# Attention units alternated on VectorE with buffers of their own, mixer tiles re-ordered, and the reciprocal root moved to ScalarE, in a fused attention and gated-MLP block

## The chip, the cores and the metric

The kernel runs on one core of a Trainium2 chip. The metric is the device time of one execution, in microseconds (us). Every comparison below uses executions of both kernels on the same chip in the same rounds. The runs of one kernel lie within 0.7% of each other.

The engines are TensorE (PE in the profile; its weight loads are PEld), VectorE (DVE), ScalarE (ACT), GpSimd (POOL) and SyncE (SP, which issues all DMA transfers of the kernel before, and all but the 16 `o` stores of the kernel after).

## The reference

The input x is 2048 rows by 1024 columns, in bfloat16. The reference, cut to what matters:

```python
def _A_ref(x, wqkv, wo):                 # local dilated attention: 32 heads of 32, window 8, dilation 2
    qkv = (x @ wqkv) ...                 # 1024 -> 3072
    idx = pos[:, None] - off[None, :]    # each row sees itself and 7 earlier rows, two apart
    logits = einsum('bhsd,bhswd->bhsw', q, kg) * scale
    attn = softmax(where(mask, logits, -1e9))
    o = einsum('bhsw,bhswd->bhsd', attn, vg)
    return o @ wo

def _B_ref(x, w_in, w_sp, b_sp, w_out):  # gated MLP with a mix over rows
    z = gelu(x @ w_in)                   # 1024 -> 3584
    z1, z2 = z[..., :1792], layernorm(z[..., 1792:])
    g = einsum('ts,bsf->btf', w_sp, z2) + b_sp[None, :, None]   # 2048 x 2048
    return (z1 * g) @ w_out

h = x + _A_ref(layernorm(x))
out = h + _B_ref(layernorm(h))
```

## The kernel before

There are three stages.

- **Stage A** normalises x, does the QKV matmul for 16 tiles of 128 rows and stores the result to DRAM. VectorE does the attention from there, in 8 "pairs". For each pair it does four QK units (a product and a tree of adds), a softmax with its Exp on ScalarE, and four AV units. The result `o` goes to DRAM.
- **Stage B** works in four blocks of four tiles. Block c needs the attention of pairs 2c and 2c+1. For each tile, S1 transposes the attention result, S2 multiplies by wo and collects statistics, S3 normalises, S4 transposes, S5 computes z2 with gelu, and Z1 computes z1 with gelu.
- **Stage C** mixes over all rows and multiplies by w_out. The change doesn't touch it.

Stages A and B on one side and the attention on the other are two Python generators, "main" and "att". Each `yield t` advances its virtual clock by t, and the generator with the lower clock emits next. That, and then the framework's own scheduler, sets the order in which instructions stand on each engine. The parts that the change touches, cut:

```python
# attention on VectorE
def D1(i):                                     # QK
    for hh in range(2):
        for r in range(2):
            prod = att1.tile([P, W, 512], BF16, name="prod", tag="prod")      # att1: one buffer per tag
            tmp  = att1.tile([P, W, 256], BF16, name="tmp", tag="tmp")
            nc.vector.tensor_tensor(prod[:], qh..., ek[:, r:r + W, :], ALU.mult)              # L482
            nc.vector.tensor_tensor(tmp[:], prod[:, :, 0:256], prod[:, :, 256:512], ALU.add)  # L484
            ...                                # four more halving adds, the last one writes lg
            yield 5.4
def D2(i):                                     # softmax, first half
    nc.vector.tensor_reduce(mx[:], ..., AX.X, ALU.max)
    nc.vector.tensor_tensor(lg[:], lg[:], mx..., ALU.subtract)
    nc.scalar.activation(lg[:], lg[:], AF.Exp)                                # L498
def D3(i):                                     # AV
    pr2 = att1.tile([P, W, 512], BF16, name="pr2", tag="prod")                # the same buffer as prod
    nc.vector.tensor_tensor(pr2..., at..., ev..., ALU.mult)                   # L519
    ...                                        # three halving adds, the last one writes o
    nc.sync.dma_start(dap(o_d[c], ...), os_[r][:])
# order: D1(i), D2(i), D3(i-1), D4(i) (second half of the softmax), D1(i+1), ...

# stage B, in each S2(m), after the matmuls of its tile
nc.scalar.activation(hn[:], h_t[:], AF.Square, bias=nm[:], accum_out=ssq[:])
nc.scalar.activation(ssq[:], ssq[:], AF.Identity, bias=eps_t[:], scale=1.0 / D)
nc.gpsimd.tensor_tensor(rs[:], ssq[:], neghalf[:, 0:1], ALU.pow)              # L365, root on GpSimd
# order in a block: S1 S2 (tile 0), S1 S2 (tile 1), Z1 of two tiles left from the block before,
# S3(0) S4(0) S3(1); then for each tile m: S5(m), S1(m+2), S2(m+2), Z1(m), S4(m+1), S3(m+2)
```

Of the kernel before, what the change touches and what calls it, by code (L numbers as in the profile page):

```python
# [48 lines left out]
def kernel(  # L49
# [12 lines left out]
    nc = tc.nc  # L62
# [26 lines left out]
    mask0 = const.tile([P, 2, W, H], F32, name="mask0")  # L89
# [68 lines left out]
    def gen_main():  # L158
        order = [(c, jj) for c in range(NC) for jj in (0, 2, 1, 3)]
        pbl = abctx.enter_context(tc.tile_pool(name="pbl", bufs=2))  # L160
        with ExitStack() as actx:
# [7 lines left out]
            def Lload(a):  # L169
                if a >= NT:  # L170
                    return
                c, jj = order[a]
                x_t = pa.tile([P, D], BF16, name="x_t", tag="x_t", bufs=6)
                nc.sync.dma_start(x_t[:], dap(x2d, 512 * c + jj, 0, [[4, P], [1, D]]))  # L174
                xts[a] = x_t

            def Lstats(a):
                if a >= NT:
                    return
                xn = pa.tile([P, D], BF16, name="xn", bufs=3)  # L180
# [25 lines left out]
            def Ldve(a):  # L206
# [9 lines left out]
                xn = pa.tile([P, D], BF16, name="xn", bufs=3)  # L216
# [9 lines left out]
            for n in range(1, 6):  # L226
                nc.sync.dma_start(wqkv_sb[:, :, n * 512:(n + 1) * 512], wq_v[:, :, n * 512:(n + 1) * 512])
                if n <= 3:
                    Lload(n + 1)
# [4 lines left out]
            yield 8.0  # L234
# [26 lines left out]
            for a in range(NT):  # L261
                for n in range(6):
                    if n == 0:
                        Lload(a + 5)
                        if a + 2 >= NDVE:
                            Lstats(a + 2)
# [7 lines left out]
                    yield 1.85  # L274
# [15 lines left out]
        with ExitStack() as bctx:  # L290
            wI = bctx.enter_context(tc.tile_pool(name="wI", bufs=1))
            pb = bctx.enter_context(tc.tile_pool(name="pb", bufs=2))
            win1_sb = wI.tile([P, KD, Fh], BF16, name="win1_sb")
            pend_z1 = []

# [11 lines left out]
            for c in range(NC):  # L307
# [8 lines left out]
                ons, xrs, oTs, hts, hns, hTs, ln2, z2s = {}, {}, {}, {}, {}, {}, {}, {}  # L316
                sz = small.tile([P, 4, NFC], F32, name="sz")
                v3 = small.tile([P, 4], F32, name="v3")

                def Bload(m):  # L320
# [3 lines left out]
                    o_n = pbl.tile([P, D], BF16, name="o_n")  # L324
                    nc.sync.dma_start(o_n[:], o_d[c][m * P:(m + 1) * P, :])
                    x_r = pbl.tile([P, D], BF16, name="x_r")
# [9 lines left out]
                def S1(m):  # L336
                    pt = pe_transposes(ons.pop(m))
                    oT = pb.tile([P, KD, P], BF16, name="oT")
                    evac(oT, pt)
                    oTs[m] = oT  # L340

                def S2(m):
                    t = 4 * c + m
                    oT, x_r = oTs.pop(m), xrs.pop(m)
                    h_t = pb.tile([P, D], BF16, name="h_t", bufs=3)
                    hts[m] = h_t
                    s1p = small.tile([P, 2], F32, name="s1p")
                    for n in range(2):
# [4 lines left out]
                        nc.tensor.matmul(ps[:], lhsT=ident[:], rhs=x_r[:, n * 512:(n + 1) * 512], start=False, stop=True)  # L353
                        nc.scalar.activation(h_t[:, n * 512:(n + 1) * 512], ps[:], AF.Identity, accum_out=s1p[:, n:n + 1])
                    nc.sync.dma_start(h_d[t][:, :], h_t[:])
                    Bload(m + 2)
                    nm = small.tile([P, 1], F32, name="nm2")
                    j2 = small.tile([P, 2], F32, name="j2")
                    nc.scalar.activation(j2[:], s1p[:], AF.Identity, scale=-1.0 / D, accum_out=nm[:])
                    hn = pb.tile([P, D], BF16, name="hn")  # L360
                    ssq = small.tile([P, 1], F32, name="ssq2")
                    nc.scalar.activation(hn[:], h_t[:], AF.Square, bias=nm[:], accum_out=ssq[:])
                    nc.scalar.activation(ssq[:], ssq[:], AF.Identity, bias=eps_t[:], scale=1.0 / D)
                    rs = small.tile([P, 1], F32, name="rs2")
                    nc.gpsimd.tensor_tensor(rs[:], ssq[:], neghalf[:, 0:1], ALU.pow)  # L365
                    ln2[m] = (nm, rs, hn)

                def S3(m):
                    nm, rs, hn = ln2.pop(m)
                    nb = small.tile([P, 1], F32, name="nb2")  # L370
                    if last:
                        nc.vector.tensor_tensor(nb[:], nm[:], rs[:], ALU.mult)
                        nc.vector.tensor_scalar(hn[:], hts.pop(m)[:], rs[:], nb[:], ALU.mult, ALU.add)
                    else:
                        nc.scalar.mul(nb[:], nm[:], rs[:])
                        nc.scalar.activation(hn[:], hts.pop(m)[:], AF.Identity, bias=nb[:], scale=rs[:])
                    hns[m] = hn

                def S4(m):
                    pt = pe_transposes(hns.pop(m))  # L380
# [4 lines left out]
                def S5(m):  # L385
                    t = 4 * c + m
                    hT = hTs[m]
                    z2t = z2n[:, t, :] if last else pb.tile([P, ZP], BF16, name="z2s", bufs=4)
                    z2s[m] = z2t
                    for n2 in range(NFC):  # L390
                        ps = ps_mm.tile([P, 512], F32, name="ps", tag="ps")
                        for k in range(KD):
                            nc.tensor.matmul(ps[:, 0:FC], lhsT=hT[:, k, :], rhs=win2_sb[:, k, n2 * FC:(n2 + 1) * FC],  # L393
                                             start=(k == 0), stop=(k == KD - 1))
                        zc = z2t[:, n2 * FC:(n2 + 1) * FC]
# [11 lines left out]
                Bload(0)  # L407
                Bload(1)
# [8 lines left out]
                S2(0)  # L417
                yield 4.5
                S1(1)
                S2(1)  # L420
                yield 4.5
                while pend_z1:
                    yield from Z1(*pend_z1.pop(0))
                S3(0)
                S4(0)
                S3(1)
                yield 1.0
                for m in range(4):
                    yield from S5(m)
                    if m + 2 < 4:  # L430
                        S1(m + 2)
                        S2(m + 2)
                        yield 4.5
# [4 lines left out]
                    if m + 1 < 4:  # L438
                        S4(m + 1)
                        yield 0.6  # L440
                    if m + 2 < 4:
                        S3(m + 2)
                nc.scalar.activation(v3[:], v3[:], AF.Identity, bias=eps_t[:], scale=1.0 / Fh)
                nc.gpsimd.tensor_tensor(rstd3[:, 4 * c:4 * c + 4], v3[:], neghalf[:, 0:4], ALU.pow)  # L444
                yield 1.0
                if last:
                    load_wT(0)
# [4 lines left out]
    def gen_att():  # L452
        NPAIR = 2 * NC
        eks, qhs, evs, lgs, ats = {}, {}, {}, {}, {}

        def loadK(i):
            c, pi = i // 2, i % 2
            base = cls_d[c][pi]
            for hh in range(2):
                qh = att.tile([P, 2, 512], BF16, name="qh")  # L460
                nc.sync.dma_start(qh[:], dap(base, HALO, hh * 512, [[2, P], [1, 2], [1, 512]]))
                ek = att.tile([P, W + 1, 512], BF16, name="ek")
                nc.sync.dma_start(ek[:], dap(base, 0, D + hh * 512, [[2, P], [1, W + 1], [1, 512]]))
                qhs[i, hh], eks[i, hh] = qh, ek

        def loadV(i):
            c, pi = i // 2, i % 2
            base = cls_d[c][pi]
            for hh in range(2):
                ev = att.tile([P, W + 1, 512], BF16, name="ev")  # L470
                nc.sync.dma_start(ev[:], dap(base, 0, 2 * D + hh * 512, [[2, P], [1, W + 1], [1, 512]]))
                evs[i, hh] = ev

        def D1(i):
            lg = att.tile([P, 2, W, H], F32, name="lg")
            lgs[i] = lg
            for hh in range(2):
                qh, ek = qhs.pop((i, hh)), eks.pop((i, hh))
                for r in range(2):
                    prod = att1.tile([P, W, 512], BF16, name="prod", tag="prod")  # L480
                    tmp = att1.tile([P, W, 256], BF16, name="tmp", tag="tmp")
                    nc.vector.tensor_tensor(prod[:], qh[:, r, :].unsqueeze(1).to_broadcast([P, W, 512]),  # L482
                                            ek[:, r:r + W, :], ALU.mult)
                    nc.vector.tensor_tensor(tmp[:], prod[:, :, 0:256], prod[:, :, 256:512], ALU.add)  # L484
                    nc.vector.tensor_tensor(prod[:, :, 0:128], tmp[:, :, 0:128], tmp[:, :, 128:256], ALU.add)  # L485
                    nc.vector.tensor_tensor(tmp[:, :, 0:64], prod[:, :, 0:64], prod[:, :, 64:128], ALU.add)
                    nc.vector.tensor_tensor(prod[:, :, 0:32], tmp[:, :, 0:32], tmp[:, :, 32:64], ALU.add)
                    nc.vector.tensor_tensor(lg[:, r, :, hh * 16:(hh + 1) * 16], prod[:, :, 0:16], prod[:, :, 16:32], ALU.add)
                    yield 5.4

        def D2(i):
# [4 lines left out]
            nc.vector.tensor_reduce(mx[:], lg[:].rearrange("p r j h -> p r h j"), AX.X, ALU.max)  # L496
            nc.vector.tensor_tensor(lg[:], lg[:], mx[:].unsqueeze(2).to_broadcast([P, 2, W, H]), ALU.subtract)
            nc.scalar.activation(lg[:], lg[:], AF.Exp)  # L498
            yield 2.1

        def D4(i):
            lg = lgs.pop(i)
            sm = small.tile([P, 2, H], F32, name="sm")
            nc.vector.tensor_reduce(sm[:], lg[:].rearrange("p r j h -> p r h j"), AX.X, ALU.add)
# [4 lines left out]
            yield 2.4  # L509

        def D3(i):
            c, pi = i // 2, i % 2
            at = ats.pop(i)
            os_ = [att.tile([P, D], BF16, name="o", tag="o", bufs=3) for _ in range(2)]
            for hh in range(2):
                ev = evs.pop((i, hh))
                for r in range(2):
                    pr2 = att1.tile([P, W, 512], BF16, name="pr2", tag="prod")
                    nc.vector.tensor_tensor(pr2[:].rearrange("p j (d hl) -> p j d hl", hl=16),  # L519
# [125 lines left out]
```

## Time and profile before

| what | before | where it is read |
|---|---|---|
| time | 811.31 us, median of 6 (809.84 to 812.87) | runs |
| TensorE busy | 748.7 of 808.0 us | engine table of the page |
| TensorE reaches the last block of stage B | 430.95 us | timeline of TensorE |
| TensorE starts stage C | 513.51 us | timeline of TensorE |
| last attention operation on VectorE | ends at 413.8 us | timeline of VectorE |

The engine table of the page of the kernel before gives busy time, share of the span and number of instructions:

```profile
PE 748.7 (93%) x3936; PEld 372.4 (46%) x3936; DVE 465.8 (58%) x535; ACT 324.6 (40%) x702; POOL 26.8 (3%) x32
```

TensorE is busy nearly all the time, so a gain must come from its gaps and from matmuls that run slowly. The windows view of the same kernel splits the span into the time before the last block of stage B, that block, and stage C. The columns are the window, its length, busy time and instructions of TensorE, its weight loads, VectorE, ScalarE and GpSimd, then the clock that TensorE was granted (1.00 is full speed), the DMA share and GB/s:

```profile
20.00:430.95 410.95, 369.00 (x1960) 181.87 (x1959) 344.15 (x365) 274.75 (x578) 18.32 (x14) 0.96 0.73 235
430.95:513.50 82.55, 80.50 (x457) 41.93 (x456) 14.66 (x19) 46.89 (x121) 4.23 (x6) 1.00 0.38 109
513.50:808.00 294.50, 290.77 (x1472) 143.93 (x1471) 96.67 (x125) 0.00 (x0) 0.00 (x0) 1.00 0.46 116
```

The last two windows have no idle TensorE worth speaking of (2.1 of 82.6 us and 3.7 of 294.5 us). The first has 42 us of it. Its gaps of 2 us and more are in the timeline of TensorE. Columns here and in every timeline are start, duration, engine, line, operation, output and inputs, sizes, count; the bracket has the idle time before it and what ended it:

```profile
98.57 1.03 PE L144 MATMUL pt<-ident,xn 128*128 128x128 bf16 x8 [5.88 <-ACT xn L195]
...
215.25 3.60 PE L351 MATMUL ps<-wo_sb,oT 128*128 128x512 bf16 x8 [13.92 <-DMA win_sb<-in_B_w_in_dram]
...
248.79 6.23 PE L393 MATMUL ps<-win_sb,hT 128*128 128x448 bf16 x32 [3.07 <-ACT hT L148]
...
322.18 7.85 PE L393 MATMUL ps<-win_sb,hT 128*128 128x448 bf16 x32 [2.07 <-ACT hT L148]
...
343.52 1.03 PE L144 MATMUL pt<-ident,hn 128*128 128x128 bf16 x8 [3.10 <-ACT hn L376]
```

For the longest the profile names a DMA of weights that this matmul doesn't read. The timeline of ScalarE shows what held it: the copy that makes `oT`, which the matmul does read, waited 13.1 us for a store of QKV results.

```profile
214.19 1.93 ACT L148 COPY oT<-pt 128x1024 bf16<-128x1024 bf16 x2 [13.09 <-DMA cls_d<-qkv_sb]
```

The timeline of VectorE shows how one QK unit runs. Each operation reads what the one before it wrote:

```profile
128.18 2.29 DVE L482 TENSOR_TENSOR prod<-qh,ek 128x4096 bf16<-128x4096 bf16 x1
130.50 1.23 DVE L484 TENSOR_TENSOR tmp<-prod 128x2048 bf16<-128x2048 bf16 x1
131.76 0.69 DVE L485 TENSOR_TENSOR prod<-tmp 128x1024 bf16<-128x1024 bf16 x1
```

From one start to the next it is 2.32 us for an operation of 2.29 us, and 1.26 us for one of 1.23 us. There is a pause of about 0.03 us after each.

The waits view lists, for an engine's instruction at a line, what it waited for, the total, the number of waits and the longest. Three of its lines for the kernel before:

```profile
PE ps L393 <- ACT hT L148: 11.0, 9, 3.1
ACT lg L498 <- DVE lg L497: 12.2, 5, 7.5
SPq L527 <- DVE o L524: 55.7, 13, 8.4
```

The second is the Exp, waiting for VectorE. The third is the DMA queue holding an `o` store that waits for VectorE.

Last, the groups of instructions by line, for GpSimd: the root in stage B, and the same operation early on, before VectorE is busy.

```profile
L365 POOL TENSOR_TENSOR rs<-ssq,neghalf 128x1 f32<-128x1 f32 x16 | 17.8, 1109 | 380.1 <-ACT ssq L363 363.2 <-issue 16.9
L215 POOL TENSOR_TENSOR brs<-brs,neghalf 128x1 f32<-128x1 f32 x4 | 2.4, 607 | 14.3 <-DVE brs L214 14.3
```

### The profile page before, as it was taken

What the parts mean: (1) busy time and instruction counts of PE and PEld (TensorE: products, weight loads), DVE (VectorE), ACT (ScalarE), POOL (GpSimd) and SP (SyncE); (2) the same over time, 40 slices, a digit from 0 to 9 for tenths busy, and PEclk for the clock granted to TensorE, in tenths of its full rate; (3) what the DMA queues carried; (4) which work ended last, traced back from release to release, by engine and by line L of the source; (5) the groups of instructions that cost most, each with busy time, mean ns of one, the idle gap of its engine ahead of it and who ended that gap; (6) DMA issues with size and microseconds to landing.
All of it is one profiled execution on the core that took longest, in us unless ns stands there. A gap on an engine that the chain in (4) does not pass through costs nothing.

```text
span 808.0 us, 9851 instructions
## 1 busy us (share of the span) xinstructions
PE 748.7 (93%) x3936; PEld 372.4 (46%) x3936; DVE 465.8 (58%) x535; ACT 324.6 (40%) x702; POOL 26.8 (3%) x32
## 2 busy tenths in 40 slices
PE   4899799999388898899999999999999999999998
PEld 2444344444144444444554555444444444444443
DVE  5048899999999999998941000443333333334222
ACT  1857495843197686668677465100000000000000
POOL 2000000000000021101001000000000000000000
PEclk9999899999699999989999999999999999999999
DMA  9669996958796776563649510594443335554111
GB/s 298 187 236 171 368 286 228 316 178 306 280 288 206 235 251 216 184 201 104 231 159 333 153 50 24 200 280 125 108 98 98 97 100 124 119 109 132 42 37 49
DMA packets 144721, 145.58 MB, mean 180 GB/s; under 512 B 69058, under 2 KB 116218, under 8 KB 144676
## 3 DMA queue, kind: packets, MB, share of 16 engines
q1 hardware_dynamic: 144676, 144.97, 59.7%
q8 instruction: 30, 0.49, 0.3%
q14 instruction: 15, 0.12, 0.0%
HBM read 90.97 MB, written 38.24 MB: 160 GB/s over the span
## 4 chain that ended last, share of the span: by engine, by line
PE 59%; DVE 25%; ACT 6%; DMA 5%; SPq 2%; issue 2%; POOL 1%; POOLq 0%; DVEq 0%
PE psg L579 24%; PE pso L598 12%; PE ps L393 9%; DVE prod L482 6%; PE ps L301 5%; DVE pr L519 5%; PE ps L351 4%; PE ps L245 4%; DVE tmp L484 3%; DVE pr L522 2%; DVE prod L485 2%; DMA wqkv_sb<-in_A_wqkv_dram 2%; DVE pr L523 1%; SPq L174 1%; DMA ek<-cls_d 1%
## 5 line engine op out<-in xcount | busy, mean ns | idle before, releaser
L579 PE MATMUL psg<-z2n,wT 128*128 128x448 bf16 (+1 forms) x1024 | 196.4, 353 | 0.6 <-ACT z1s L303 0.6
L245 PE MATMUL ps<-wqkv_sb,xT 128*128 128x512 bf16 x768 | 171.4, 383 | 4.2 <-DMA wqkv_sb<-in_A_wqkv_dram 2.4
L579 PEld LDWEIGHTS <-wT 128*128 128x128 bf16 x1024 | 100.2, 98 | 95.3 <-issue 0.9
L245 PEld LDWEIGHTS <-xT 128*128 128x128 bf16 x768 | 75.2, 99 | 94.5 <-issue 6.5
L393 PE MATMUL ps<-win_sb,hT 128*128 128x448 bf16 x512 | 102.6, 361 | 12.0 <-ACT hT L148 11.0
L583 DVE SCALAR_TENSOR_TENSOR u<-psg,bc,z_c 128x448 bf16<-128x448 f32 x64 | 43.6, 683 | 107.6 <-PE psg L579 101.1
L598 PE MATMUL pso<-wout_sb,uT 128*128 128x512 bf16 x448 | 99.1, 379 | 0.0
L301 PE MATMUL ps<-win_sb,hT 128*128 128x448 bf16 x512 | 98.8, 352 | 0.0
L482 DVE TENSOR_TENSOR prod<-qh,ek 128x4096 bf16<-128x4096 bf16 x32 | 73.4, 2293 | 17.3 <-DMA ek<-cls_d 16.3
L247 ACT ACTIVATE qkv_sb<-ps 128x512 bf16<-128x512 f32 x96 | 54.4, 595 | 60.0 <-PE ps L245 49.8
L393 PEld LDWEIGHTS <-hT 128*128 128x128 bf16 x512 | 50.1, 100 | 61.3 <-ACT hT L148 12.6
L351 PE MATMUL ps<-wo_sb,oT 128*128 128x512 bf16 x256 | 62.5, 388 | 15.8 <-DMA win_sb<-in_B_w_in_dram 13.9
L519 DVE TENSOR_TENSOR pr<-at,ev 128x4096 bf16<-128x4096 bf16 x32 | 73.3, 2289 | 0.7
L301 PEld LDWEIGHTS <-hT 128*128 128x128 bf16 x512 | 50.1, 98 | 47.3
L598 PEld LDWEIGHTS <-uT 128*128 128x128 bf16 x448 | 43.8, 98 | 52.1
L568 DVE TENSOR_TENSOR wT<-wT,rstd 128x2048 bf16<-128x2048 bf16 x16 | 36.5, 2291 | 29.9 <-POOL rstd L444 16.5
L600 DVE TENSOR_TENSOR o_t<-pso,h_c 128x512 bf16<-128x512 f32 x32 | 22.0, 689 | 44.4 <-PE pso L598 44.4
L351 PEld LDWEIGHTS <-oT 128*128 128x128 bf16 x256 | 25.2, 100 | 46.8 <-ACT oT L148 15.9
L484 DVE TENSOR_TENSOR tmp<-prod 128x2048 bf16<-128x2048 bf16 x32 | 39.2, 1225 | 1.1
L303 ACT ACTIVATE z1s<-ps 128x448 bf16<-128x448 f32 x64 | 33.0, 536 | 15.8 <-PE ps L301 15.3
L522 DVE TENSOR_TENSOR pr<-pr 128x2048 bf16<-128x2048 bf16 x32 | 38.9, 1215 | 0.7
L396 ACT ACTIVATE z2s<-ps 128x448 bf16<-128x448 f32 x48 | 26.0, 542 | 33.1 <-PE ps L393 33.1
(84 smaller groups left out, 495.5 us busy)
## 6 DMA issues: line engine op xcount, KB each, us to landing
ek<-cls_d SPq DMA_DIRECT2D x16, 1152.0 KB
ev<-cls_d SPq DMA_DIRECT2D x16, 1152.0 KB
cls_d<-qkv_sb SPq DMA_DIRECT2D x16, 768.0 KB
win_sb<-in_B_w_in_dram SPq DMA_DIRECT2D x16, 448.0 KB
z_d<-z1s SPq DMA_DIRECT2D x16, 448.0 KB
z_c<-z_d SPq DMA_DIRECT2D x16, 448.0 KB
wqkv_sb<-in_A_wqkv_dram SPq DMA_DIRECT2D x6, 1024.0 KB
z_d<-z2s SPq DMA_DIRECT2D x12, 448.2 KB
```

What stands on the lines that cost most here:

```text
L245: nc.tensor.matmul(ps[:], lhsT=xT[:, k, :], rhs=wqkv_sb[:, k, n * 512:(n + 1) * 512], start=(k == 0), stop=(k == KD - 1))
L247: nc.scalar.activation(qkv_sb[:, n * 512:(n + 1) * 512].rearrange("p (d hl) -> p d hl", hl=16), ps[:].rearrange("p (hl d) -> p d hl", d=Dh ...
L301: nc.tensor.matmul(ps[:, 0:FC], lhsT=hT[:, k, :], rhs=win1_sb[:, k, n * FC:(n + 1) * FC], start=(k == 0), stop=(k == KD - 1))
L351: nc.tensor.matmul(ps[:], lhsT=oT[:, k, :], rhs=wo_sb[:, k, n * 512:(n + 1) * 512], start=(k == 0), stop=False)
L393: nc.tensor.matmul(ps[:, 0:FC], lhsT=hT[:, k, :], rhs=win2_sb[:, k, n2 * FC:(n2 + 1) * FC], start=(k == 0), stop=(k == KD - 1))
L482: nc.vector.tensor_tensor(prod[:], qh[:, r, :].unsqueeze(1).to_broadcast([P, W, 512]), ek[:, r:r + W, :], ALU.mult)
L484: nc.vector.tensor_tensor(tmp[:], prod[:, :, 0:256], prod[:, :, 256:512], ALU.add)
L519: nc.vector.tensor_tensor(pr2[:].rearrange("p j (d hl) -> p j d hl", hl=16), at[:, r, :, hh * 16:(hh + 1) * 16].unsqueeze(2).to_broadcast( ...
L522: nc.vector.tensor_tensor(pr2[:, 0:4, :], pr2[:, 0:4, :], pr2[:, 4:8, :], ALU.add)
L579: nc.tensor.matmul(ps[:, 0:w_], lhsT=wT[:, k, :], rhs=z2n[:, k, n * FC:n * FC + w_], start=(k == 0), stop=(k == NT - 1))
L583: nc.vector.scalar_tensor_tensor(u[:, n * FC:(n + 1) * FC], ps[:, 0:FC], bc[:], z1[:, n * FC:(n + 1) * FC], ALU.add, ALU.mult)
L598: nc.tensor.matmul(ps[:], lhsT=uT[:, k, :], rhs=wout_sb[:, k, n * 512:(n + 1) * 512], start=(k == 0), stop=(k == KF - 1))
```

## The change

The change means to remove TensorE's gaps before stage C and to make VectorE's attention flow. It has five parts, which came together:

1. The pools of stage B wait tile by tile for the space they take over, not for the whole pool before them.
2. Attention is alternated unit by unit (QK of one pair, AV of the pair before, five units apart). AV gets a buffer of its own. K and V are loaded by halves, and V earlier. Exp is emitted 2 us later. The `o` stores go to GpSimd's DMA queue. Smaller pools elsewhere make the room.
3. In stage B all four tiles are loaded up front and go through S2 first. Their roots are taken together ("episode"). S1 of the next tile stands inside S2, and S3 and S4 of later tiles stand inside S5.
4. The reciprocal root is a ScalarE function instead of a GpSimd power.
5. Max and sum of the softmax are three tensor operations each instead of a reduce.

Some yields and buffer counts changed with them.

The core of the diff, cut:

```diff
-    mask0 = const.tile([P, 2, W, H], F32, name="mask0")
+    mask0 = const.tile([P, 2, W, H], BF16, name="mask0")
-                x_t = pa.tile([P, D], BF16, name="x_t", tag="x_t", bufs=6)      # xn: bufs 3 -> 2
+                x_t = pa.tile([P, D], BF16, name="x_t", tag="x_t", bufs=4)
-            wI = bctx.enter_context(tc.tile_pool(name="wI", bufs=1))
-            pb = bctx.enter_context(tc.tile_pool(name="pb", bufs=2))
+            wI = bctx.enter_context(tc.tile_pool(name="wI", bufs=1, reuse_waits="tile"))
+            pb = bctx.enter_context(tc.tile_pool(name="pb", bufs=2, reuse_waits="tile"))
 ...
-                    nc.gpsimd.tensor_tensor(rs[:], ssq[:], neghalf[:, 0:1], ALU.pow)
+                def rsqrt_act(dst, src, n):
+                    nc.scalar.activation(dst, src, AF.Abs_reciprocal_sqrt, bias=eps_t[:], scale=1.0 / n)
+                def episode(m0, m1):
+                    rsqrt_act(rs4[:, m0:m1], rs4[:, m0:m1], D)
+                    if pend_v3: ...                       # the z2 root of the block before, in the same place
+                    for m in range(m0, m1):
+                        nc.scalar.mul(nm4[:, m:m + 1], nm4[:, m:m + 1], rs4[:, m:m + 1])
 ...
+                    for m in range(4):                    # blocks 1 to 3; block 0 in two halves
+                        S2(m)                             # S2 has S1(m + 1) inside
+                        yield 4.5
+                    episode(0, 4)
+                    S3(0)
+                    S4(0)
+                    S3(1)
                 while pend_z1:
                     yield from Z1(*pend_z1.pop(0))
                 for m in range(4):
                     yield from S5(m)                      # S5 has S4(m + 1) and S3(m + 2) inside
-                    (S1(m + 2), S2(m + 2), S4(m + 1), S3(m + 2) here)
 ...
+        def AV(i, u):
-                    pr2 = att1.tile([P, W, 512], BF16, name="pr2", tag="prod")
+            pr2 = att1.tile([P, W, 512], BF16, name="pr2", tag="pr2")
-                        nc.sync.dma_start(dap(o_d[c], 2 * r + pi, 0, [[4, P], [1, D]]), os_[r][:])
+                nc.gpsimd.dma_start(dap(o_d[c], 2 * r + pi, 0, [[4, P], [1, D]]), o[:])
+        LAG = 5
+        for g in range(NU + LAG):
+            if g < NU:
+                QK(g // 4, g % 4)
+            if g >= LAG:
+                AV((g - LAG) // 4, (g - LAG) % 4)
+            if g < NU and g % 4 == 3:
+                D2(g // 4)                                # max and subtract
+            if g < NU + 1 and g % 4 == 0 and g >= 4:
+                D4(g // 4 - 1)
+            if g < NU and g % 4 == 3:
+                yield 2.0
+                D2e(g // 4)                               # Exp
+                yield -2.0
```

## The prediction

> **What bounds it now.** The page's engine table gives TensorE 748.7 of 808.0 us. The last stage (spatial mix and output matmul) starts at 513.5 us and then runs TensorE without a gap to the end; the diff does not touch it. So everything is decided before 513.5 us.
>
> There, two engines compete. TensorE's timeline: one QKV tile takes 10.8 us (16 tiles, 173 us), one mixer tile about 16.9 us (0.44+3.9+0.44+6.06+6.06; 16 tiles, 270 us): 443 us of work from 13.4 us on. Its listed gaps sum to 44 us: 13.9 at 201-215 (ScalarE's first oT copy waits 13.1 us for the last qkv_sb store), 5.9 at 93-99, 3.1 at 249, 2.1 at 322, 3.1 at 343, and many of about 1. By windows the granted clock falls to 0.52-0.84 after the long gaps; I estimate 9 us from lengthened matmul groups (14.3 for 12.3, 7.85 for 6.23). VectorE runs attention from 51.1 to 412 us with only 9.8 us of waits (4.5 for ek, 1.7+1.5+2.1 for Exp, all in its timeline). A pair of attention tiles costs it about 44 us.
>
> **What the change does.**
> 1. Per-tile reuse waits: oT, h_t and the new loads would overlie the QKV weights, free at the last QKV matmul, not the stored qkv_sb. The 13.9 us gap and about 2.5 us of slow clock should shrink to about 2 us.
> 2. Exp issued later on ScalarE, o_d stores taken off the SP queue (it waited 55.7 us there for VectorE), K and V loaded by halves and V earlier: fewer blocked stores; the 93-99 gap should shrink, perhaps half of it.
> 3. Next-tile normalize, transpose and copy put inside the S5 matmuls: most of the 11.0 us of hT waits and 5.0 us of hn waits go. In return four S2 in a row, then statistics, table load and normalize: about 7 us of latency per block, mostly filled by the two pending Z1 (12 us).
> 4. Reciprocal root on ScalarE in place of POOL: removes 1.1 us operations, adds about ten table switches at 1.28 us. [...] this trace has 1283. ScalarE then is about 90% busy in a mixer block, so some new short gaps.
> 5. Max and sum as three tensor operations in place of a 1.04 us reduce: estimate 0.93 us. Almost nothing. Interleaving QK and AV units removes the Exp waits.
>
> **Critical path.** TensorE alone could reach the last stage at about 480. But its last block needs all attention: VectorE ends at about 406 (51+351+4 of waits), store and reload as now 6 us: 412. Then four S2 18, statistics latency 7, four S5+Z1 50: 487. So the VectorE path takes over as the binding one, and of 53 us of TensorE loss only about 26 is realised.
>
> **Predicted: 785 us, range 774 to 798.** Chances: faster 0.83, same 0.14, slower 0.03.
>
> **Signs.** Step 1: no TensorE gap over 3 us near 200. Step 3: TensorE waits on hT under 4 us, on hn small. Path: VectorE ends at 402-410; first psg matmul at 482-493; the last stage still 295 us long. More table loads, about 20 in place of 10.
>
> **What would make it wrong.** POOL-queued stores starving while VectorE runs ([...] here the POOL power takes 1109 ns beside busy VectorE, 607 before it) would delay each block. Fewer x_t and xn buffers could starve QKV. Long statistics gaps before S4 would lower the clock again. If so: about 800. If pending Z1 fill everything and attention ends earlier: about 775.

No term of its sum is cut: 412 + 18 + 7 + 50 = 487 us for the start of stage C, and 785 us for the whole execution. Its 7 us of statistics latency, its 0.93 us for a max or a sum and its 90% for ScalarE are estimates. In the kernel after, the three operations of a max take 0.41 + 0.28 + 0.21 = 0.91 us (L529 to L531), and ScalarE was busy for 51.7 of 59.2 us (87%) from 270.8 to 330 us. That the granted clock is low after a gap shows in four of five cases of the kernel before: it was 0.50 from 215.25 to 218 us (after a gap of 13.92 us), 0.50 from 98.57 to 101 (after 5.88), 0.52 from 322 to 325 (after 2.07) and 0.50 from 343.5 to 346 (after 3.10), but 1.00 from 248.79 to 252 (after 3.07).

## The result, and the profile after

The median is 795.09 us (794.11 to 795.82, 8 runs) against 811.15 us for the kernel before (808.38 to 813.94, 16 runs). The ratio is 0.9803, with a 95% interval of 0.9788 to 0.9819. A ratio here is the mean time of one kernel's runs over that of the other's runs of the same rounds, so it isn't quite the ratio of the medians. The kernel after is about 16 us faster. The interval lies clear of 1. Whether the gain reaches 2% is unclear, because the interval holds values on both sides of that. The prediction said 26.

The engine table and the three windows of the kernel after:

```profile
PE 747.0 (94%) x3936; PEld 371.3 (47%) x3936; DVE 443.1 (56%) x563; ACT 339.7 (43%) x708; POOL 13.1 (2%) x28
```

```profile
20.00:415.79 395.79, 367.44 (x1971) 181.13 (x1969) 322.52 (x398) 282.94 (x577) 8.82 (x16) 0.97 0.78 253
415.79:497.50 81.71, 80.15 (x457) 41.86 (x456) 14.04 (x15) 54.29 (x128) 0.00 (x0) 1.00 0.17 59
497.50:792.00 294.50, 290.77 (x1472) 143.96 (x1471) 96.79 (x125) 0.00 (x0) 0.00 (x0) 1.00 0.44 116
```

This table holds the whole result. Stage C is as long as before to a tenth. The last block of stage B is 81.7 us in place of 82.6. All else is that TensorE reaches the last block at 415.8 in place of 431.0. So from here on a kernel can be judged by one number: **when TensorE reaches the last block**. In all runs below but one, 81.7 to 82.6 us of stage B follow, and in all of them 294.5 to 294.8 us of stage C. The exception is e10, with 90.0 us: there the scheduler put 32 matmuls of the block before (6.2 us) after this point. The table of the experiments therefore gives the start of stage C.

Within the time before stage C, TensorE's idle time fell from 44.0 to 29.9 us (length minus busy time of the first two windows), and its busy time by 1.9 us.

The gaps that are left, from the timeline of TensorE:

```profile
94.46 0.62 PE L144 MATMUL pt<-ident,xn 128*128 128x128 bf16 x8 [4.09 <-ACT xn L195]
...
125.99 12.22 PE L245 MATMUL ps<-wqkv_sb,xT 128*128 128x512 bf16 x48 [4.81 <-ACT xT L148]
...
245.73 4.78 PE L395 MATMUL ps<-win_sb,hT 128*128 128x448 bf16 x16 [4.29 <-ACT z1s L304]
...
355.42 3.27 PE L357 MATMUL ps<-wo_sb,oT 128*128 128x512 bf16 x8 [6.46 <-ACT oT L148]
```

The 13.9 us gap is gone, and so are those on hT and hn. Three new ones, at 126, 246 and 355, all end with something from ScalarE. The timeline of ScalarE shows why, here for the last of them:

```profile
346.16 1.28 ACT L535 ACT_TABLE_LOAD   x1
353.65 0.63 ACT L535 ACTIVATE lg<-lg 128x512 f32<-128x512 f32 x1 [6.22 <-DVE lg L532]
...
354.38 0.99 ACT L148 COPY oT<-pt 128x1024 bf16<-128x1024 bf16 x1
```

ScalarE has the Exp next in its order. It loads the table and waits 6.2 us for VectorE. The copy that TensorE needs stands behind the Exp. The waits view sums this up. The first line is the Exp, and the other two are what the new order of stage B did to the waits on hT and hn:

```profile
ACT lg L535 <- DVE lg L532: 20.7, 5, 6.2
...
PE pt L144 <- ACT hn L376: 1.0, 2, 0.5
...
PE ps L395 <- ACT hT L148: 0.9, 1, 0.9
```

The timeline of VectorE after the change, for one AV unit and one QK unit:

```profile
131.38 2.29 DVE L514 TENSOR_TENSOR pr<-at,ev 128x4096 bf16<-128x4096 bf16 x1
133.58 2.29 DVE L499 TENSOR_TENSOR prod<-qh,ek 128x4096 bf16<-128x4096 bf16 x1
135.78 1.22 DVE L517 TENSOR_TENSOR pr<-pr 128x2048 bf16<-128x2048 bf16 x1
136.92 1.22 DVE L501 TENSOR_TENSOR tmp<-prod 128x2048 bf16<-128x2048 bf16 x1
```

The two chains alternate. From one start to the next it is now 2.20 us for the 2.29 us operation (2.32 before), and 1.14 us for the 1.22 us operation (1.26 before). Most of the pauses of about 0.03 us are gone: an operation starts before the one ahead has ended (at 133.58 us, when the one ahead ends at 133.67). About 0.12 us is saved at each. The attention has 320 such operations (32 QK units of six, 32 AV units of four), so this is worth up to 38 us, an estimate. The last attention operation ends at 375.7 us in place of 413.8, which is 40 us before TensorE reaches the last block.

### The profile page after: what moved, and what is told of

It is laid out like the page before. It is cut to its first block, busy times and chain, and to the rows that moved or that the text cites. A ratio compares the mean times of both kernels' runs of the same rounds, so it can differ in the third digit from the quotient of the medians. Undisturbed runs are those within 1.5% of the kernel's fastest.

```text
span 792.3 us, 9858 instructions
## 1 busy us (share of the span) xinstructions
PE 747.0 (94%) x3936; PEld 371.3 (47%) x3936; DVE 443.1 (56%) x563; ACT 339.7 (43%) x708; POOL 13.1 (2%) x28
## 4 chain that ended last, share of the span: by engine, by line
PE 58%; DVE 34%; ACT 3%; issue 2%; DMA 2%; SPq 1%; DVEq 0%
PE psg L623 24%; PE pso L642 12%; DVE prod L499 8%; DVE pr L514 8%; PE ps L395 6%; PE ps L302 5%; PE ps L245 5%; DVE tmp L501 4%; DVE pr L517 4%; PE ps L357 3%; DVE prod L502 2%; DVE pr L518 1%; DVE tmp L503 1%; PE pt L144 1%; DVE o L519 1%
## 5 line engine op out<-in xcount | busy, mean ns | idle before, releaser
L245 PE MATMUL ps<-wqkv_sb,xT 128*128 128x512 bf16 x768 | 174.6, 389 | 6.4 <-ACT xT L148 4.8
L612 DVE TENSOR_TENSOR wT<-wT,rstd 128x2048 bf16<-128x2048 bf16 x16 | 36.5, 2291 | 25.5 <-ACT rstd L414 13.4
```

The source lines that it names most:

```text
L245: nc.tensor.matmul(ps[:], lhsT=xT[:, k, :], rhs=wqkv_sb[:, k, n * 512:(n + 1) * 512], start=(k == 0), stop=(k == KD - 1))
```

## The experiments

Twelve kernels ran. Times are medians in us, beside the kernel before in the same rounds. Runs of different rounds are compared below as they stand; the kernel before differed by 0.3 us at most between them.

| run | this | before | ratio (95%) | TensorE starts stage C |
|---|---|---|---|---|
| after | 795.09 | 811.15 | 0.9803 (0.9788 to 0.9819) | 497.51 |
| e1 before + tile-wise waits | 808.59 | 811.15 | 0.9971 (0.9947 to 0.9994) | 512.74 |
| e2 after, pool-wise waits | 794.82 | 811.15 | 0.9796 (0.9776 to 0.9816) | 498.62 |
| e3 after, shared buffer | 808.49 | 811.15 | 0.9966 (0.9947 to 0.9985) | 511.87 |
| e4 after, Exp tied to later work | 789.23 | 811.15 | 0.973 (0.9713 to 0.9746) | 492.83 |
| e5 after, Exp waits for nothing (wrong result) | 784.57 | 811.42 | 0.9673 (0.9647 to 0.97) | 487.94 |
| e6 before + own buffer | 852.38 | 811.42 | 1.0515 (1.0484 to 1.0547) | 554.93 |
| e7 after, `o` stores on SP | 795.0 | 811.42 | 0.9801 (0.9778 to 0.9824) | 498.87 |
| e8 after, root on GpSimd | 827.57 | 811.42 | 1.0203 (1.0179 to 1.0228) | 530.58 |
| e9 after, root on GpSimd, shared buffer | 808.8 | 811.17 | 0.9965 (0.9933 to 0.9997) | 511.05 |
| e10 before + own buffer, root on ScalarE | 811.4 | 811.17 | 0.9999 (0.9984 to 1.0014) | 515.92 |
| e11 after + tied Exp + stores on GpSimd's queue | 785.34 | 811.17 | 0.9678 (0.9663 to 0.9692) | 489.03 |
| e12 the same, other distances | 778.41 | 811.11 | 0.96 (0.9572 to 0.9629) | 481.38 |

### The buffer of its own (e3)

The theory was that the separate buffer lets VectorE alternate two chains, and that this speed is needed. The rival was that VectorE ends earlier because of earlier loads and removed Exp waits. The edit, on the kernel after:

```diff
-            pr2 = att1.tile([P, W, 512], BF16, name="pr2", tag="pr2")
+            pr2 = att1.tile([P, W, 512], BF16, name="pr2", tag="prod")
```

> The changed kernel, but the products of AV share the one buffer of the products of QK again, so the two chains cannot alternate inside VectorE. Theory (VectorE finished at 376 us rather than at my 406 because independent operations of two chains follow each other about 0.1 us closer than dependent ones): VectorE ends at 400 to 412 us and the time rises to 800 to 808 us. Rival (VectorE ends earlier because of earlier loads and removed Exp waits): it still ends at 376 to 382 us and the time stays within 2 us of 795.

It took 808.49 us, so 13.4 of the 16 us were lost again. VectorE's attention ended at 415.3 us, as late as in the kernel before. Both lie just past the ranges of the theory and far from the rival. The waits view shows TensorE waiting for attention results, in three blocks:

```profile
PE pt L144 <- DMA o_n<-o_d: 30.2, 3, 12.0
```

In the kernel after, this line is 1.4 us. So the buffer matters, though VectorE had 40 us to spare at the last block. The slack there is not the slack elsewhere: the three waits are at 210, 274 and 360 us, when the earlier blocks are due.

### Waits by tile or by pool (e1 and e2)

One adds the first part of the change to the kernel before, and the other takes it from the kernel after. The edit of e1 (e2 is its reverse on the kernel after):

```diff
-            wI = bctx.enter_context(tc.tile_pool(name="wI", bufs=1))
-            pb = bctx.enter_context(tc.tile_pool(name="pb", bufs=2))
+            wI = bctx.enter_context(tc.tile_pool(name="wI", bufs=1, reuse_waits="tile"))
+            pb = bctx.enter_context(tc.tile_pool(name="pb", bufs=2, reuse_waits="tile"))
```

> The kernel before, with the per-tile reuse waits alone. Theory: the 13.9 us TensorE gap at 201-215 us shrinks to under 3 us, but because VectorE still ends near 412 us and the third attention block still arrives near 350 us, only part of it is kept: total 800 to 807 us. Rival (the gap is worth its whole length plus the slow clock after it): about 795 us. Rival 2 (the gap comes from the late store of the last qkv_sb in the SP queue, not from the pool's wait): the gap stays, 811 us.

> The changed kernel with the per-tile reuse waits taken back. Theory: a TensorE gap of 8 to 15 us returns between the last QKV tile and the first oT use, and the time rises by 10 to 16 us, to 805 to 811 us. Rival (the rest of the change already removed the late store): under 3 us more, 795 to 798 us.

In e1 the gap of 13.9 us at 201 to 215 fell to 0.7 us. But the time fell by 2.6 us only, a little less than expected. The timeline of TensorE shows the gain given back 20 us later:

```profile
224.88 1.03 PE L144 MATMUL pt<-ident,o_n 128*128 128x128 bf16 x8 [10.78 <-DMA o_n<-o_d]
```

The loads of `o_n` stood in SP's queue behind 7.3 us of issuing weight loads. In e2 a gap of 6.25 us came back at 209 us, but the one of 4.29 us at 246 vanished, and TensorE was level again at the second block (first S2 at 270.6 in place of 270.8 us). The time was 794.82, the same as after within the interval. The theory (805 to 811 us) failed and the rival held: the rest of the change had removed over half of the gap already. So this part is worth 2.6 us alone and nothing within the change, though it removes the longest gap of the profile.

### The Exp at the head of ScalarE's order (e4 and e5)

Theory: the three new gaps come from the Exp that ScalarE reaches before VectorE has its input. In e4 each Exp gets a bias of zero that is computed from a later result of ScalarE's own main work, so it can't be placed before that work. AV follows QK by seven units in place of five, and the second half of the softmax by two units more:

```diff
         def D2e(i):
-            nc.scalar.activation(lgs[i][:], lgs[i][:], AF.Exp)
+            zb = small.tile([P, 1], F32, name="zb")
+            nc.scalar.mul(zb[:], last_act[0], 0.0)         # last_act: newest result of the main stream
+            nc.scalar.activation(lgs[i][:], lgs[i][:], AF.Exp, bias=zb[:])
-        LAG = 5
+        LAG = 7
-            if g < NU + 1 and g % 4 == 0 and g >= 4:
+            if 6 <= g < NU + 3 and g % 4 == 2:
                 D4(g // 4 - 1)
-                yield 2.0
+                yield 12.0
                 D2e(g // 4)
-                yield -2.0
+                yield -12.0
```

> The changed kernel with each Exp tied to a ScalarE result of the main stream about 12 us of schedule later, and AV and its softmax sum two units later to leave room. Theory (three of the four remaining large TensorE gaps, 4.8 us at 121-126, 4.3 at 241-246 and 6.5 at 349-355, come from an Exp that stands at the head of ScalarE's order waiting for VectorE): waits of Exp on VectorE fall from 20.7 us to under 5, the gaps go, 775 to 786 us. Rival (ScalarE is simply full with its 23 table loads): the gaps stay elsewhere, 793 to 797 us.

It took 789.23 us, 5.9 less than the kernel after, but not the 775 to 786 that were expected. ScalarE's waits for VectorE at the Exp fell only to 12.2 us (one of 9.3 and one of 2.9). VectorE in turn waited for the Exp and ended at 393.5. TensorE waited for attention at 211 us (4.64 us). The direction was right. The size was missed, because the delay moves the wait to VectorE where it is too long.

In e5 the Exp works on a constant tile and waits for no VectorE result, and the softmax goes without it. Its result is wrong (relative error 1.15):

```diff
-            nc.scalar.activation(lgs[i][:], lgs[i][:], AF.Exp)
+            zb = small.tile([P, 1], F32, name="zb")
+            nc.scalar.mul(zb[:], last_act[0], 0.0)
+            nc.scalar.activation(zrow[:], zrow[:], AF.Exp, bias=zb[:], scale=0.0)
```

> The changed kernel with a deliberately wrong result: each Exp works on a constant tile and the softmax goes on without it, so ScalarE does the same work and table loads but never waits for VectorE inside attention. Theory (an Exp at the head of ScalarE's order, waiting for VectorE, makes the gaps of 4.8, 4.3 and 6.5 us and the slow clock after them): these gaps go, time 774 to 785 us. Rival (ScalarE full of work and table loads): within 3 us of 795.

It took 784.57 us, 10.5 less than the kernel after. That is about what the Exp costs by standing at the head of ScalarE's order. (VectorE's own waits for the Exp, 3.5 us, go as well in this run.) It is not 20.7 us, the sum of the waits. Only three of the five waits left a long gap on TensorE, and a new gap of 6.01 us came at 312 us, where ScalarE waited 11.9 us for a z1 buffer whose store stood in SP's queue.

### Where the `o` stores go (e7)

The kernel after with the `o` stores back on SP's queue:

```diff
-                nc.gpsimd.dma_start(dap(o_d[c], 2 * r + pi, 0, [[4, P], [1, D]]), o[:])
+                nc.sync.dma_start(dap(o_d[c], 2 * r + pi, 0, [[4, P], [1, D]]), o[:])
```

> The changed kernel with the o_d stores back on the SP queue. My prediction's step 2 says that these stores blocked other transfers there: SP again waits some 50 us for VectorE, and the time rises by 2 to 8 us. Rival (it is off the critical path): within 2 us of 795.

It took 795.0 us: no effect, as the rival said. Gaps moved (4.39 us at 207, 4.25 us at 234 us), and TensorE's idle time before stage C was 31.1 us beside 29.9. SP waited 57.5 us for `o` again, and it cost nothing in this setting. On GpSimd's queue the stores took 0.54 us to issue and landed in 3.4 us (median).

### The root on GpSimd (e6, e8, e9, e10)

The plan for e6 was to measure the separate buffer by itself, on the kernel before. It has the smaller pools of the change too, which make the room for the buffer:

```diff
-                    pr2 = att1.tile([P, W, 512], BF16, name="pr2", tag="prod")
+                    pr2 = att1.tile([P, W, 512], BF16, name="pr2", tag="pr2")
 ... and mask0 in bfloat16, x_t bufs 6 -> 4, xn bufs 3 -> 2, Lload(a + 4), as in the change
```

> The kernel before with only a separate buffer for the AV products, paid for by the smaller x_t and xn pools and the bf16 mask as in the change. Theory (the buffer is what lets the two chains alternate on VectorE): VectorE's attention ends 25 to 36 us earlier, at 376 to 388 us; but the gap at 201-215 and TensorE's other gaps stay, so the time falls by at most 8 us, to 803 to 811. Rival (VectorE was the bound): 785 to 800.

It took 852.38 us, 41 us *more* than the kernel before, far outside both ranges. Attention ended at 438.8 us, not 376 to 388. The framework's scheduler alternated the QK and AV chains by itself as soon as the buffers allowed it. The timeline of GpSimd shows what that did to the root, an operation on one element per partition:

```profile
220.36 15.85 POOL L365 TENSOR_TENSOR rs<-ssq,neghalf 128x1 f32<-128x1 f32 x1 [201.22 <-ACT ssq L363]
242.26 0.55 POOL L365 TENSOR_TENSOR rs<-ssq,neghalf 128x1 f32<-128x1 f32 x1 [6.05 <-ACT ssq L363]
...
356.47 26.57 POOL L365 TENSOR_TENSOR rs<-ssq,neghalf 128x1 f32<-128x1 f32 x1 [19.59 <-ACT ssq L363]
```

The same operation takes 0.55 us or 26.57 us. Spans on GpSimd are rough, but the waits of TensorE bear them out. TensorE waits for the result by way of ScalarE. Its timeline, at the end of the longest one:

```profile
384.70 1.03 PE L144 MATMUL pt<-ident,hn 128*128 128x128 bf16 x8 [25.60 <-ACT hn L376]
```

During the root of 15.85 us 21 VectorE operations ran, and 29 during that of 26.57 us, none of them longer than 2.29 us.

The theory that came of this: a root on GpSimd takes long while VectorE runs its operations back to back, without the pauses. The kernel before would be safe by the 0.03 us pauses between dependent operations (no root took over 2.3 us there). e8 puts the root of the kernel after back on GpSimd. It, before this theory, was expected at 792 to 799 us. If the theory is right, e8 must be slow, the root must be harmless there when the buffer is shared (e9), and the loss of e6 must go when the root moves to ScalarE (e10). The rival was that the root is slow for another reason, such as its place in the order. The edits:

```diff
e8, on the kernel after:
-                    nc.scalar.activation(dst, src, AF.Abs_reciprocal_sqrt, bias=eps_t[:], scale=1.0 / n)
+                    nc.scalar.activation(dst, src, AF.Identity, bias=eps_t[:], scale=1.0 / n)
+                    nc.gpsimd.tensor_tensor(dst, dst, neghalf[:, 0:dst.shape[-1]], ALU.pow)
e9: e8 and the shared buffer of e3
e10, on e6:
-                    nc.scalar.activation(ssq[:], ssq[:], AF.Identity, bias=eps_t[:], scale=1.0 / D)
-                    nc.gpsimd.tensor_tensor(rs[:], ssq[:], neghalf[:, 0:1], ALU.pow)
+                    nc.scalar.activation(rs[:], ssq[:], AF.Abs_reciprocal_sqrt, bias=eps_t[:], scale=1.0 / D)
 ... and the root of z2 in the same way
```

> The changed kernel with the reciprocal root back on POOL. Theory: 8 of the 23 table loads and about 5 gelu reloads go, 12 to 17 us of ScalarE work, but they lie mostly in slack; POOL adds a round trip of 2 to 4 us before each normalization: 792 to 799 us. Rival (table loads are what holds the changed kernel back): 780 to 788 us.

> The changed kernel with both the reciprocal root back on POOL and the one shared product buffer. Theory (POOL's power waits for a moment in which VectorE has a gap, and only the alternating chains leave none): the POOL powers last at most 3 us again, as before, against 22 us in the run with separate buffers, and the time is 803 to 815 us, less than that run's 827.6 although VectorE is slower. Rival (the power is slow for another reason, such as its place in the order): powers of over 10 us again and 825 us or more.

> The kernel before with the separate AV buffer and, besides, its reciprocal roots on ScalarE, still one per tile. Theory (the buffer was harmful alone only because it starved POOL): the loss of 41 us turns into a gain; VectorE ends at 376 to 390 us; TensorE keeps the gap near 200 and short gaps, and some 16 more table switches cost ScalarE about 40 us: 795 to 812 us. Rival (the buffer alone is harmful in the old order for other reasons as well): 820 us or more.

With e3 and the kernel after, these make a square, in us:

| on the order of the kernel after | root on ScalarE | root on GpSimd |
|---|---|---|
| own buffer | 795.1 (after) | 827.6 (e8) |
| shared buffer | 808.5 (e3) | 808.8 (e9) |

With the shared buffer the engine of the root makes no difference. With the own buffer it makes 32 us, so e8 missed both ranges that were on record for it. (The round trip of 2 to 4 us in its expectation was an estimate. In the kernel before, four of them at 241 to 298 us took 1.2 to 2.1 us from the end of L363 to the start of L375.) The timelines of GpSimd and of TensorE in e8 show the two longest roots and the waits that follow them:

```profile
217.13 22.14 POOL L415 TENSOR_TENSOR rs<-rs,neghalf 128x2 f32<-128x2 f32 x1 [13.69 <-ACT rs L414]
...
307.37 22.66 POOL L415 TENSOR_TENSOR rs<-rs,neghalf 128x4 f32<-128x4 f32 x1 [9.17 <-ACT rs L414]
```

```profile
243.15 1.04 PE L144 MATMUL pt<-ident,hn 128*128 128x128 bf16 x8 [21.40 <-ACT hn L376]
...
332.11 1.03 PE L144 MATMUL pt<-ident,hn 128*128 128x128 bf16 x8 [22.75 <-ACT hn L376]
```

During each of these two roots 27 VectorE operations ran, none longer than 2.31 us. In e9 no root took more than 2.61 us. VectorE's operations followed each other more slowly with the shared buffer (of the 53 operations of 2.29 us between 85 and 378 us, 40 are followed after 2.32 or 2.33 us in e3, and 45 after 2.20 or 2.21 us in e8 with own buffers), and yet the kernel was 19 us faster than e8. This agrees with the theory and not with the rival. In e10 the 41 us of e6 are gone (811.4 us).

But e10 is not faster than the kernel before, though its attention ends 27 us earlier, at 386.5. A gap of 12.3 us at 213 is still there, and ScalarE has 41 table loads in place of 10. The time lies in the expected range, but the gain that the theory spoke of did not come. Whether VectorE's speed is worth something in the old order of stage B isn't shown, because the added table loads (31 of 1.28 us on ScalarE) came with it. All the rest of the change, without the own buffer and with the root on GpSimd, is worth 2.4 us (e9 against before). Everything together is worth 16.

What ends a long root stays open. In e6 the two longest roots end at 236.21 and 383.04, each 0.37 us after the small pause between two dependent operations on VectorE (at 235.84 and 382.67 us). The two longest of the kernel before, of 2.23 and 2.28 us, end 0.37 us after such a pause too. But not every long root ends so. A third root of e6, of 11.74 us, ends without one at 336.88, 0.49 us after a TENSOR_REDUCE has started (336.39). In e8 no such pause stands out either: all four roots over 2.4 us end 0.6 to 0.9 us after the last operation of a max or a sum, one of the shortest on VectorE there (0.22 to 0.24 us). No run separates these cases.

### Better versions (e11 and e12)

Both tie Exp to later main work as in e4, but with a distance for each pair of tiles, and put the stores of qkv, h, z1 and z2 on GpSimd's queue too. e12 differs from e11 in the distances alone. Its edit on the kernel after, with the tied Exp as in e4 left out:

```diff
+        KS = (0, 0, 1, 1, 1, 1, 1, 1)                      # e11: (0, 1, 1, 1, 2, 2, 2, 2)
+        YS = (2.0, 2.0, 8.0, 8.0, 8.0, 8.0, 8.0, 8.0)      # e11: (2, 8, 8, 8, 12, 12, 12, 12)
-            ga = g - LAG
-            if ga >= 0:
+            ga = na                                        # na: AV units emitted so far
+            if ga < NU and g >= ga + 5 + KS[ga // 4]:
+                na += 1
 ... D4 comes KS units later as well, and Exp YS us later in place of 2.0
-                nc.sync.dma_start(z1_d[t][:, :], z1s[:])
+                nc.gpsimd.dma_start(z1_d[t][:, :], z1s[:])
 ... and so for the stores of qkv, h and z2
```

> Towards a better version: the changed kernel with each Exp from the second pair on tied to a later ScalarE result of the main stream (8, later 12 us of schedule), AV one and later two units further behind, and the z1, z2, h and QKV stores on the POOL queue, away from the loads that wait for VectorE. Theory (what is left is in-order blocking on ScalarE by Exp, about 10 us by the run with free Exps, and on the SP queue): 776 to 786 us. Rival (the POOL queue delays the stores beside a VectorE without gaps): 790 us or more.

> The best try with less distance: only one unit more between Exp and AV from the third pair on, none for the first two. In the best try TensorE waited 6.4 and 5.6 us for o_n, that is for VectorE's finished attention. Theory (the added distance delays attention by one unit, 5 us, at those points): these two waits shrink by 3 to 6 us each unless an Exp wait comes back; 776 to 785 us. Rival (Exp waits come back in the same measure): 784 to 790 us.

e11 took 785.34 us and e12 778.41 us (777.22 to 780.22), with the right result. e12 is 16.7 us below the kernel after and beats both kernels. Its stores on GpSimd's queue landed in 7.6 us (qkv), 2.9 (z1) and 6.1 (z2), medians. Its windows and its longest gap, from the timeline of TensorE:

```profile
20.00:399.73 379.73, 361.99 (x1969) 179.56 (x1966) 322.16 (x398) 283.14 (x585) 41.31 (x77) 0.99 0.76 252
399.73:481.40 81.67, 80.17 (x458) 41.88 (x457) 14.07 (x15) 54.29 (x128) 5.40 (x10) 1.00 0.36 122
```

```profile
206.09 1.03 PE L144 MATMUL pt<-ident,o_n 128*128 128x128 bf16 x8 [7.11 <-DMA o_n<-o_d]
```

The last block is as long as ever. TensorE reaches it at 399.7 us in place of 415.8. The granted clock of the first window rose from 0.97 to 0.99 with the gaps gone, and TensorE's busy time there fell by 5.5 us. The longest wait left is for the attention of the first block. There the expectation failed: of the two waits of e11 that were to shrink, the one of 5.6 us went, but the one of 6.4 us is now 7.1. No run separates the tied Exp from the moved stores in e11 and e12.

## Why the prediction was right or wrong

**Right:** the direction, and the range (774 to 798), the latter partly by luck, as point 2 shows. Stage C kept its 295 us. No gap over 3 us stands near 200. The waits on hT fell from 11.0 to 0.9 us and on hn from 5.0 to 1.0. Table loads rose from 10 to 23. For the cost of one the prediction took 1.28 us, and the loads in both traces take 1283 ns each. In the kernel after, the load at 343.97 us starts 0.02 us after the operation before it has ended, and its activation starts 1.30 us after the load did (345.27). The 16 stores on GpSimd's queue did not starve: they took 0.54 us to issue and 3.4 us to land (medians), nearly all beside a busy VectorE.

**Wrong in size.** It said 785 us and stage C at 487 (482 to 493 as a sign); measured were 795.1 and 497.5. The prediction added up a path: VectorE ends at 406, store and reload until 412, then "four S2 18, statistics latency 7, four S5+Z1 50". Two of its terms failed, and so did its choice of the path.

1. *"statistics latency 7".* The last block took 81.7 us, not 75. In the timeline of TensorE, the part with S1 and S2 takes 17.9 us (415.8 to 433.7). The two Z1 left over, with a transpose among them, take 13.3 us (to 446.95). S5, Z1 and the transposes take 49.9 us, and a wait of 0.6 us ends it. The prediction put 7 where 13.3 stands: it knew that two pending Z1 of 6 us each fill the time of the statistics, and counted the latency instead of the longer work that hides it. That is 6.3 of the 10.5 us. The kernel before would have given the right sum, because its last block took 82.6 us.
2. *"So the VectorE path takes over as the binding one", "VectorE ends at about 406".* VectorE ended at 375.7, and TensorE reached the last block 40 us later, at 415.8, held by its own gaps. The prediction took the alternation of QK and AV for "almost nothing". It saved about 0.12 us at each operation, and e3 shows that this comes from the separate buffer. The late end that was predicted and the TensorE time that was missed happened to lie 3.8 us apart (412 and 415.8), so the total looks nearer than the reasons were. That is luck. For attention that ends earlier the prediction had foreseen about 775; attention ended 30 us earlier than it said, and the time was 795.1.
3. *"TensorE alone could reach the last stage at about 480".* Less the 81.7 us of the last block, this is an arrival at 398. Measured was 415.8. The term left out is ScalarE's order: the Exp ahead of the copies, 20.7 us of waits. Without them (e5) TensorE reaches the last block at 406.2 and the time falls by 10.5 us. The other 8 us are not traced to a cause. The prediction wrote "Interleaving QK and AV units removes the Exp waits". VectorE waits less for the Exp (3.5 in place of 5.3 us), but ScalarE waits more for VectorE (20.7 in place of 12.2). It looked at one end of the handshake only. e12, with further edits, reaches the last block at 399.7, so the room was real. The change didn't take it.
4. *Step 1* removed the gap that it said it would, and it was worth little: 2.6 us alone (e1), none within the change (e2). *Step 2* said that the gap at 93 to 99 us would shrink, "perhaps half of it". It is 5.7 us in two parts (4.09 and 1.60) in place of 5.9. Taking the `o` stores off SP's queue was worth nothing (e7).
5. *Step 4* was read as a small trade, 1.1 us operations against table switches. It is what the rest stands on: with the root left on GpSimd, the same kernel takes 827.6 us (e8). The prediction took the root's 1109 ns beside a busy VectorE and 607 ns before it as the sign of a danger for stores on GpSimd's queue. That danger did not come true (3.4 us to land, and 795.0 us with the stores back on SP's queue against 795.1, e7). The two numbers were the root's own, with up to 2.28 us beside a busy VectorE, and the root is where the danger was.

**What stays open.** No run measures the new order of stage B by itself, and the scheduler reorders other instructions with every edit, so a few us of each difference may be order and not cause. Nor do the runs show what ends a long root on GpSimd.

## What to carry to other kernels

Two independent chains on VectorE ran closer here when each had a buffer of its own (2.20 us from start to start for the 2.29 us operation, 2.32 before), but a root on GpSimd beside them then took up to 26.57 us in place of 0.55, so move such operations off the critical path first. An instruction that waits for another engine held what stood behind it in its engine's order (here the Exp waited 6.22 us, and the copy that TensorE needed came after it): look at both ends of every handshake, and place it behind work that is sure to be ready. A removed gap is worth only what the next wait leaves, so ask when the bottleneck reaches a fixed point near the end, and check the deadline of every block and not that of the last one alone.
